# Requesting the q weights earlier and in two pieces: the order of the first loads in a fused attention and GLU kernel

## The chip, the cores and the metric

One core of a Trainium2 chip. The metric is the time of one execution on the device in microseconds (us), lower is better; medians of several runs are quoted with their range. The span in a profile is some 1.7 us shorter than the time of the same run, because it counts from the first to the last instruction. Ratios are computed as the mean time of one kernel's fast runs over the mean of the other's of the same rounds, so they are not quite the ratio of the medians quoted beside them.

## The reference, cut to what matters

A layer norm of x (2048 rows of 512, bf16), then a local dilated attention (32 heads of 16, eight keys for each position) and a gated GLU on the same normalized x, combined at the end:

```python
x = A_x
xn = _layernorm(x, axis=-1)
s = _A_ref(xn, A_wqkv, A_wo)                      # q, k, v projections, attention, wo
g = _silu(_B_ref(xn, B_w_gate, B_w_up, B_w_down)) # gelu(xn@wg) * (xn@wu) @ wd
return x + s * g
```

For this change only the beginning matters: the first 512 rows of x (tiles 0 to 3 of 128 rows) must be loaded, normalized and transposed, and the q and k weights (the first two 512-column blocks of `wqkv`, 512 KB each) must be there, before TensorE can project.

## The kernel before: the parts concerned

All loads are issued by one queue in this order (cut):

```python
    def load_w(dst, src, lo, hi):
        nc.sync.dma_start(
            out=dst[:, :, lo:hi], in_=src.rearrange("(k p) n -> p k n", p=P)[:, :, lo:hi]
        )

    for t in range(TPQ - 1):
        load_x(t)                       # x tiles 0, 1, 2: 128 KB each
    load_w(wqkv_sb, A_wqkv, 0, D)       # q weights: 512 KB
    load_x(TPQ - 1)                     # x tile 3
    for i in range(1, 3):
        load_w(wqkv_sb, A_wqkv, i * D, (i + 1) * D)   # k, v weights
    load_x(TPQ, TPQ)                    # x tiles 4 to 7
    ...                                 # GLU weights and the rest of x
```

And the beginning of the compute (cut). `project` makes the matmuls, four row blocks (`dks`) of weights for each group; `transpose` transposes a normalized tile on TensorE and copies the result out of PSUM:

```python
    first_moments(0); first_moments(1)          # one statement a line in the kernel
    first_normalize(0)
    transpose(0)
    first_normalize(1)
    warm_up(4, P)
    transpose(1, parts=2)                       # copied out by ScalarE, in two parts
    warm_up(4, P)
    first_moments(2); first_moments(3)
    first_normalize(2); first_normalize(3)
    ...
    for dks in ((0, 1), (2, 3)):                # q for tiles 0 and 1
        for fo in range(NC):
            project(qs[fo], wqkv_sb, fo * P, 0, 0, HQ, dks)
    for fo in range(NC):
        qkv(0, fo, 0, HQ, qs[fo])
    transpose(HT, copy=nc.vector.tensor_copy)   # tile 2
    for fo in range(NC, 2 * NC):                # k for tiles 0 and 1
        qkv(0, fo, 0, HQ)
        if fo == NC:
            transpose(HT + 1, copy=nc.vector.tensor_copy)   # tile 3
    ...
    for fo in range(2 * NC):                    # q and k for tiles 2 and 3
        qkv(0, fo, HQ, HQ)
```

The softmax here doesn't subtract the row's maximum and nothing guards it: scores larger than these inputs give would overflow.

Of the kernel before, what the change touches and what calls it, by code (L numbers as in the profile page):

```python
# [13 lines left out]
P = 128  # L14
# [14 lines left out]
def kernel(  # L29
# [13 lines left out]
    nc = tc.nc  # L43
    B, S, D = A_x.shape
    DF = B_w_gate.shape[1]
    NT, NC, NF, NJ = S // P, D // P, DF // P, S // TQ
    TPQ = TQ // P
# [28 lines left out]
    wqkv_sb = wts.tile([P, NC, 3 * D], BF16, name="wqkv_sb")  # L76
# [7 lines left out]
    def load_x(t, n=1):  # L84
        nc.sync.dma_start(  # L85
            out=x_sb[:, t : t + n, :],
            in_=x2d[t * P : (t + n) * P, :].rearrange("(t p) d -> p t d", p=P),
        )

    def load_w(dst, src, lo, hi):  # L90
        nc.sync.dma_start(
            out=dst[:, :, lo:hi], in_=src.rearrange("(k p) n -> p k n", p=P)[:, :, lo:hi]
        )

    for t in range(TPQ - 1):
        load_x(t)
    load_w(wqkv_sb, A_wqkv, 0, D)
    load_x(TPQ - 1)
    for i in range(1, 3):
        load_w(wqkv_sb, A_wqkv, i * D, (i + 1) * D)  # L100
    load_x(TPQ, TPQ)
    for i, (lo, hi) in enumerate(((0, DF // 2), (DF // 2, DF))):
        load_w(wg_sb, B_w_gate, lo, hi)
        load_w(wu_sb, B_w_up, lo, hi)
        load_x((2 + i) * TPQ, TPQ)

    def load_late_weights():
# [16 lines left out]
        out=vT.rearrange("(k p) n -> p k n", p=P)[:, :, 0:PAD],  # L124
        in_=zpad[:],
# [82 lines left out]
    def transpose(t, parts=1, copy=None):  # L208
        xn = xns[t]
        tr = mm.tile([P, NC * P], BF16, name="tr", tag="mm")  # L210
        for c in range(NC):
            nc.tensor.transpose(tr[:, c * P : (c + 1) * P], xn[:, c * P : (c + 1) * P], ident[:])  # L212
        j, i = divmod(t, TPQ)
        if i == 0:
            xnT[j] = xtp.tile([P, NC, TQ], BF16, name="xnT")
        dst = xnT[j][:, :, i * P : (i + 1) * P]
        src = tr[:].rearrange("p (c n) -> p c n", c=NC)
        for k in range(parts):
            c = slice(k * NC // parts, (k + 1) * NC // parts)
            if copy is None:  # L220
                nc.scalar.activation(out=dst[:, c], in_=src[:, c], func=AF.Copy)  # L221
            else:
                copy(out=dst[:, c], in_=src[:, c])

    def warm_up(n, cols):

        ps = mm.tile([P, TQ], F32, name="warm_ps", tag="mm")
        for _ in range(n):
            nc.tensor.matmul(
                ps[:, 0:cols], lhsT=nc.const_aps.tensor(1.0, [P, P], BF16),  # L230
                rhs=nc.const_aps.tensor(1.0, [P, cols], BF16), start=True, stop=True,
            )
# [24 lines left out]
    def qkv(j, fo, i0=0, n=TQ, ps=None):  # L257
        which, c = divmod(fo, NC)
        if fo == 0 and i0 == 0:
            st[j]["q"] = qp.tile([P, NC, TQ], BF16, name="q_sb")  # L260
        if ps is None:
            ps = mm.tile([P, n], F32, name="qkv_ps", tag="mm")[:]
            project(ps, wqkv_sb, fo * P, j, i0, n)
        if which == 0:
            nc.scalar.activation(out=st[j]["q"][:, c, i0 : i0 + n], in_=ps, func=AF.Copy)  # L265
        elif which == 1:
            lo = PAD + j * TQ + i0
            nc.scalar.activation(out=k_sb[:, c, lo : lo + n], in_=ps, func=AF.Copy)  # L268
        else:
            vst = sm4.tile([P, TQ], BF16, name="vst")  # L270
            nc.scalar.activation(out=vst[:], in_=ps, func=AF.Copy)  # L271
            lo = PAD + j * TQ
            nc.sync.dma_start(out=vT[c * P : (c + 1) * P, lo : lo + TQ], in_=vst[:])
# [174 lines left out]
    for i in range(TPQ):  # L448
        at(("qkv", 0, i), normalize, TPQ + i)
        at(("glu", 0, 7 + i), moments, 2 * TPQ + i)  # L450
        if i < 2:
            at(("glu", 0, i), transpose, TPQ + i)
        at(("glu", 0, 8 + i), normalize, 2 * TPQ + i)
        at(("glu", 1, 0), transpose_by_dma, 2 * TPQ + i)
        at(("glu", 1, 10 + i), moments, 3 * TPQ + i)
        at(("qkv", 2, 2 * i), normalize, 3 * TPQ + i)
        at(("glu", 2, 0), transpose_by_dma, 3 * TPQ + i)
# [31 lines left out]
    HT = TPQ // 2  # L489
# [4 lines left out]
    first_moments(1)  # L494
    first_normalize(0)
    transpose(0)
    first_normalize(1)
    warm_up(4, P)
    transpose(1, parts=2)
    warm_up(4, P)  # L500
    first_moments(2)
    first_moments(3)
# [7 lines left out]
            project(qs[fo], wqkv_sb, fo * P, 0, 0, HQ, dks)  # L510
    for fo in range(NC):
        qkv(0, fo, 0, HQ, qs[fo])
    transpose(HT, copy=nc.vector.tensor_copy)
    for fo in range(NC, 2 * NC):
        qkv(0, fo, 0, HQ)
        if fo == NC:
            transpose(HT + 1, copy=nc.vector.tensor_copy)
    for t in range(TPQ, 2 * TPQ):
        moments(t)
    sum_constants()  # L520
# [49 lines left out]
```

## Time and profile before

| | before |
|---|---|
| time, us | 230.13 (230.06 to 230.57, three runs) |
| span of the profiled run | 228.7, of a run of 230.45 |
| TensorE busy | 98% of the span |
| q weights complete | 6.95 us |
| k weights complete | 8.80 us |
| first q matmul | 7.00 us |

The profiled run is one of the slower ones of its range.

The beginning in three stretches. This is the windows view of the kernel before; the columns are the stretch, its length, then for each engine its busy time and number of instructions, the granted clock, the DMA engines' busy share and GB/s:

```profile
6.00:6.95 0.95, 0.28 (x5) 0.10 (x2) 0.38 (x2) 0.93 (x4) 0.00 (x0) 1.00 1.08 376
7.00:8.80 1.80, 1.80 (x16) 1.48 (x16) 1.37 (x5) 0.30 (x1) 0.00 (x0) 1.00 1.09 345
8.80:10.00 1.20, 1.20 (x17) 1.11 (x16) 0.93 (x4) 1.05 (x4) 0.00 (x0) 1.00 1.10 354
```

TensorE is idle for most of the stretch before 6.95, where it waits for the q weights, and not at all in the two behind it.

### The profile page before, as it was taken

The numbers are of one execution on the slowest core, as the hardware profiler recorded it, in microseconds if no ns is written. First come the engines' busy times: TensorE is split into PE (matmuls) and PEld (weight loads), VectorE is DVE, ScalarE is ACT, GpSimd is POOL, SyncE is SP. The second block draws the span as 40 slices with busy tenths as digits, with TensorE's granted clock in tenths as the row PEclk, the third lists the DMA queues.
The fourth block names the chain that finished last, engine by engine and source line by source line (L and its number), as shares of the span: only waits on it lengthen the run. The fifth ranks groups of instructions, "written<-read, shape, count | busy, mean of one in ns | idle before, by whom it ended". The sixth has DMA issues, their size and how long they took to land.

```text
span 228.7 us, 3538 instructions
## 1 busy us (share of the span) xinstructions
PE 223.6 (98%) x1324; PEld 106.3 (46%) x1324; DVE 147.6 (65%) x234; ACT 130.2 (57%) x214; POOL 23.0 (10%) x61
## 2 busy tenths in 40 slices
PE   8899999999999999999999999999999999999993
PEld 6764444444444444444444444444444444444453
DVE  4584996896995198865677169735549429945232
ACT  4679769764413866467621786747642396748211
POOL 1048973000000000110000000000000000000000
PEclk9999999999999999999999999999999999999999
DMA  6999589982378211110275711110147800000001
GB/s 163 359 373 371 140 170 199 242 204 75 109 172 197 55 24 29 26 29 0 92 175 135 170 25 28 26 34 0 45 120 165 203 26 3 0 0 4 23 23 46
DMA packets 30545, 24.46 MB, mean 107 GB/s; under 512 B 10176, under 2 KB 30528, under 8 KB 30528
## 3 DMA queue, kind: packets, MB, share of 16 engines
q1 hardware_dynamic: 30528, 24.24, 41.9%
q8 instruction: 10, 0.16, 0.3%
q14 instruction: 7, 0.06, 0.1%
HBM read 18.61 MB, written 4.31 MB: 100 GB/s over the span
## 4 chain that ended last, share of the span: by engine, by line
PE 94%; DMA 2%; ACT 1%; SPq 1%; DVE 0%; issue 0%; DVEq 0%
PE y_ps L416 21%; PE u_ps L247 21%; PE g_ps L247 21%; PE qkv_ps L247 17%; PE s_ps L426 6%; PE L_ps L304 3%; PE o_ps L375 3%; DMA wqkv_sb<-in_A_wqkv_dram 2%; PE q_ps L247 1%; ACT L400 1%; SPq L85 1%; PE den_ps L324 0%; ACT ge L400 0%; ACT vst L271 0%; PE tr L212 0%; ACT xnT L221 0%
## 5 line engine op out<-in xcount | busy, mean ns | idle before, releaser
L247 PE MATMUL g_ps<-xnT,wg_sb 128*128 128x512 bf16 x224 | 57.6, 379 | 0.0
L247 PE MATMUL u_ps<-xnT,wu_sb 128*128 128x512 bf16 x224 | 57.5, 379 | 0.0
L416 PE MATMUL y_ps<-wd_sb,h 128*128 128x512 bf16 (+1 forms) x238 | 51.2, 366 | 0.0
L404 DVE TENSOR_TENSOR h<-ge,u 128x512 bf16<-128x512 bf16 x56 | 23.8, 425 | 37.1 <-ACT u L402 36.4
L293 DVE TENSOR_TENSOR pk<-q_sb,k_sb 128x2048 bf16<-128x2048 bf16 x32 | 37.8, 1221 | 7.0 <-ACT k_sb L268 7.0
L402 ACT ACTIVATE u<-u_ps 128x512 bf16<-128x512 f32 x56 | 33.5, 599 | 14.7 <-PE u_ps L247 14.7
L400 ACT ACTIVATE ge<-g_ps 128x512 bf16<-128x512 f32 x56 | 33.5, 599 | 14.7 <-PE g_ps L247 14.4
L247 PE MATMUL qkv_ps<-xnT,wqkv_sb 128*128 128x512 bf16 (+1 forms) x208 | 40.9, 355 | 0.0
L361 DVE TENSOR_TENSOR pv<-E,v_arr 128x2048 bf16<-128x2048 bf16 x32 | 38.6, 1216 | 0.0
L416 PEld LDWEIGHTS <-h 128*128 128x128 bf16 x238 | 23.3, 98 | 25.3
L423 ACT ACTIVATE sl<-y_ps 128x512 bf16<-128x512 f32 (+1 forms) x17 | 9.7, 572 | 44.0 <-PE y_ps L416 44.0
L247 PEld LDWEIGHTS <-wu_sb 128*128 128x128 bf16 x224 | 21.9, 98 | 26.7 <-issue 0.3
L247 PEld LDWEIGHTS <-wg_sb 128*128 128x128 bf16 x224 | 21.2, 98 | 27.1 <-issue 3.0
L247 PEld LDWEIGHTS <-wqkv_sb 128*128 128x128 bf16 x224 | 21.6, 98 | 20.2 <-DMA wqkv_sb<-in_A_wqkv_dram 0.9
L434 DVE TENSOR_TENSOR m<-s_ps,sl 128x512 bf16<-128x512 f32 (+1 forms) x17 | 11.2, 658 | 24.2 <-PE s_ps L426 24.1
L426 PE MATMUL s_ps<-wo_sb,oT 128*128 128x512 bf16 (+1 forms) x68 | 16.6, 366 | 0.0
L197 POOL TENSOR_TENSOR rstd<-rstd,mhalf 128x1 f32<-128x1 f32 x12 | 7.7, 638 | 77.4 <-DVE rstd L194 75.2
L271 ACT ACTIVATE vst<-qkv_ps 128x512 bf16<-128x512 f32 x16 | 9.6, 597 | 6.4 <-PE qkv_ps L247 6.4
L268 ACT ACTIVATE k_sb<-qkv_ps 128x512 bf16<-128x512 f32 (+1 forms) x20 | 10.2, 514 | 3.5 <-PE qkv_ps L247 3.2
L265 ACT ACTIVATE q_sb<-qkv_ps 128x512 bf16<-128x512 f32 (+1 forms) x16 | 8.7, 544 | 3.6 <-PE qkv_ps L247 3.3
L426 PEld LDWEIGHTS <-oT 128*128 128x128 bf16 x68 | 6.6, 98 | 7.2
L159 POOL COPY spread<-ident 32x32 bf16<-32x32 bf16 x16 | 9.7, 646 | 0.2
(52 smaller groups left out, 115.8 us busy)
## 6 DMA issues: line engine op xcount, KB each, us to landing
v_arr<-vT SPq DMA_DIRECT2D x16, 520.0 KB, 5.1
vT<-vst SPq DMA_DIRECT2D x16, 128.0 KB, 2.1
out_dram<-o_t SPq DMA_DIRECT2D x15, 128.0 KB, 2.3
wg_sb<-in_B_w_gate_dram SPq DMA_DIRECT2D x2, 896.0 KB, 10.9
wu_sb<-in_B_w_up_dram SPq DMA_DIRECT2D x2, 896.0 KB, 12.7
wd_sb<-in_B_w_down_dram SPq DMA_DIRECT2D x1, 1792.0 KB, 13.7
wqkv_sb<-in_A_wqkv_dram SPq DMA_DIRECT2D x3, 512.0 KB, 5.6
x_sb<-in_A_x_dram SPq DMA_DIRECT2D x3, 512.0 KB, 11.4
```

The costliest lines, as they stand in the source:

```text
L159: nc.gpsimd.tensor_copy(out=spread[H * q : H * (q + 1), q, H * j : H * (j + 1)], in_=ident[H * q : H * (q + 1), H * q : H * (q + 1)],)
L247: nc.tensor.matmul(ps, lhsT=w[:, dk, lo : lo + P], rhs=xnT[j][:, dk, i0 : i0 + n], start=(dk == 0), stop=(dk == NC - 1),)
L268: nc.scalar.activation(out=k_sb[:, c, lo : lo + n], in_=ps, func=AF.Copy)
L293: nc.vector.tensor_tensor(out=pk[:], in0=st[j]["q"][:], in1=k_sb[:, :, off : off + TQ], op=ALU.mult)
L361: nc.vector.tensor_tensor(out=pv[:], in0=st[j]["E"][:, wh, :].unsqueeze(1).to_broadcast([P, 4, TQ]), in1=st[j]["va"][:, 4 * g : 4 * g + 4, ...
L400: nc.scalar.activation(out=ge[:], in_=g_ps[:], func=AF.Gelu_apprx_tanh)
L402: nc.scalar.activation(out=u[:], in_=u_ps[:], func=AF.Copy)
L404: nc.vector.tensor_tensor(out=h[:], in0=ge[:], in1=u[:], op=ALU.mult)
L416: nc.tensor.matmul(y[:], lhsT=st[j][fc][:, tt * P : (tt + 1) * P], rhs=wd_sb[:, fc, cols], start=(fc == 0), stop=(fc == NF - 1),)
L423: nc.scalar.activation(out=sl[:, cols], in_=y[:], func=AF.Silu)
L426: nc.tensor.matmul(s[:], lhsT=st[j]["oT"][:, g, tt * P : (tt + 1) * P], rhs=wo_sb[:, g, cols], start=(g == 0), stop=(g == NC - 1),)
L434: nc.vector.tensor_tensor(out=m[:], in0=s[:], in1=sl[:, cols], op=ALU.mult)
```

## The change

Its intent: let the q matmuls start earlier. The q weights move ahead of x tiles 2 and 3, in two requests (row blocks 0 and 1, then 2 and 3), so that the first half of the q matmuls needs only the first request. x tiles 2 and 3 come in one request behind them. The copy of transposed tile 1, which the q matmuls need too, is split between VectorE and ScalarE. As tile 2 now comes later, its transposes move behind the first k block.

```diff
-    def load_w(dst, src, lo, hi):
+    def load_w(dst, src, lo, hi, k0=0, k1=NC):
         nc.sync.dma_start(
-            out=dst[:, :, lo:hi], in_=src.rearrange("(k p) n -> p k n", p=P)[:, :, lo:hi]
-        )
-
-    for t in range(TPQ - 1):
-        load_x(t)
-    load_w(wqkv_sb, A_wqkv, 0, D)
-    load_x(TPQ - 1)
+            out=dst[:, k0:k1, lo:hi],
+            in_=src.rearrange("(k p) n -> p k n", p=P)[:, k0:k1, lo:hi],
+        )
+
+    load_x(0)
+    load_x(1)
+    load_w(wqkv_sb, A_wqkv, 0, D, 0, 2)
+    load_w(wqkv_sb, A_wqkv, 0, D, 2, 4)
+    load_x(2, 2)
...
-            if copy is None:
+            if copy is None or k % 2:
...
-    transpose(1, parts=2)
+    transpose(1, parts=2, copy=nc.vector.tensor_copy)
...
-    transpose(HT, copy=nc.vector.tensor_copy)
     for fo in range(NC, 2 * NC):
         qkv(0, fo, 0, HQ)
-        if fo == NC:
-            transpose(HT + 1, copy=nc.vector.tensor_copy)
+        if fo < NC + 2:
+            transpose(HT + fo - NC, copy=nc.vector.tensor_copy)
```

## The prediction

> **What bounds the kernel now.** I read, in this order: the page's busy shares, the chain that ended last in order of time, the timeline and waits of the first 12 us, and the windows view.
>
> The busy shares say TensorE:
>
> ```profile
> PE 223.6 (98%) x1324; PEld 106.3 (46%) x1324; DVE 147.6 (65%) x234; ACT 130.2 (57%) x214; POOL 23.0 (10%) x61
> ```
>
> That leaves 228.7 - 223.6 = 5.1 us of TensorE idle time in the whole span. The windows view shows where it is not:
>
> ```profile
> 24.00:200.00 176.00, 176.00 (x999) 78.36 (x998) 121.87 (x176) 103.53 (x161) 13.45 (x28) 1.00 0.41 93
> ```
>
> From 24 to 200 us TensorE has work in every moment, at clock 1.00. So a start that is earlier or later by d moves the end by d, and nothing in the middle absorbs it. The change touches only the first 12 us, so only those need to be read. The chain there:
>
> ```profile
> 0.80 0.39 SPq L85
> ...
> 1.25 0.42 SPq L85
> ...
> 1.71 0.43 SPq L85
> 2.14 0.04 issue
> 2.19 4.76 DMA wqkv_sb<-in_A_wqkv_dram
> 6.95 0.05 issue
> 7.00 1.92 PE q_ps L247 x16
> 8.91 0.31 PE tr L212 x4
> 9.22 0.44 PE qkv_ps L247 x4
> 9.66 0.22 PE tr L212 x4
> 9.88 8.27 PE qkv_ps L247 x60
> ```
>
> The first q matmul waits for the q weights (512 KB), whose request waits behind three x requests of 0.4 us each on the queue. They land at 6.95. After that the chain is TensorE alone. The timeline shows what stands close behind it:
>
> ```profile
> 6.99 1.64 PEld L247 LDWEIGHTS <-wqkv_sb 128*128 128x128 bf16 x16 [0.89 <-DMA wqkv_sb<-in_A_wqkv_dram]
> 7.00 1.92 PE L247 MATMUL q_ps<-xnT,wqkv_sb 128*128 128x256 bf16 x16 [0.72 <-DMA wqkv_sb<-in_A_wqkv_dram]
> 7.36 0.69 DVE L181 BATCH_NORM_STATS2 stats<-x_sb 128x6 f32<-128x512 bf16 x1 [0.95 <-DMA x_sb<-in_A_x_dram]
> 8.82 0.23 PEld L212 LDWEIGHTS <-xn 128*128 128x128 bf16 x4 [0.19 <-DVE xn L203]
> 9.06 0.60 PE L247 MATMUL qkv_ps<-xnT,wqkv_sb 128*128 128x256 bf16 x4
> 9.72 8.42 PE L247 MATMUL qkv_ps<-xnT,wqkv_sb 128*128 128x256 bf16 x60
> ```
>
> TensorE loses 0.72 us to the q weights. VectorE has x tile 3 only at 7.36, and tile 2's statistics (at 5.51) were finished long before. The q matmuls end as tile 2's transposes come ready: 0.19 us of waiting there. So the whole prize of an earlier q start is under one microsecond, 0.4% of the time, and other arrivals stand 0.2 us behind it.
>
> **What the Trainium skill says.** (1) "DMA: Bandwidth & Descriptors", section "Queues, rings and completion order": each DMA engine takes descriptors in ring order, and a request is complete only when all engines have counted. The trace agrees: requests land in issue order, at 2.85, 3.50 and 3.88 (x tiles 0 to 2), 6.95 (q weights), 7.34 (x tile 3), 8.80 (k weights); of the sixteen completion counts of the q weights fifteen are in by 6.32 and the last at 6.95. So order in the queue is what decides. (2) The same page, "Anatomy of one DMA", gives about 2 us fixed cost for one request (for another issuing path); here an x tile takes 2.0 to 2.2 us from issue to landing, so a second request costs nothing extra while the queue is full. (3) "VectorE: DVE Perf Modes", section "Why PSUM operands drop a tier": a PSUM operand allows at most two results a cycle. The 128x512 copies here took 424 ns, under the 533 ns that one per cycle at the page's 0.96 GHz would take: it agrees; half the columns is an estimated 424 - 133 = 290 ns. (4) "TensorE: Matmul & The Clock Gate", Part 1: the clock falls only after some 3.4 us of idleness. The granted clock is 1.00 in every window here, with the 0.72 us gap in it; the gaps expected below are shorter than 1 us, so no clock is lost.
>
> **The change part by part.**
>
> *Queue order.* Before: x0, x1, x2, q, x3, k. After: x0, x1, qA, qB, x2+x3, k; five requests ahead of k in both, so the issue time is the same. In the packet records 256 KB are done at 2.95 and 384 KB at 3.49: x2 took 0.54 us. The q weights move forward by that: complete at 6.95 - 0.54 = 6.41. Once the queue is full 128 KB takes 0.35 us, so half A (256 KB less) lands about 0.73 earlier, 5.7.
>
> *x tiles 2 and 3.* All bytes up to x3 are the same 1024 KB. x2's 128 KB now pass at the full rate (0.35 in place of 0.54), so the pair lands at 7.34 - 0.19 = 7.15 and k at 8.80 - 0.19 = 8.6. For x3 that is a gain of 0.2, but x2, which was there at 3.88, now comes at 7.15.
>
> *Copy of tile 1.* Before: ScalarE, 6.09 to 6.47 and 6.37 to 6.75. After: the first half on VectorE. Tile 1's transposes end at 6.05; tile 2's copy began 0.04 after its transposes, so 6.09 to 6.38. The built instruction order shows ScalarE's half waiting for VectorE's half: 6.40 to 6.78. It isn't shared in time; but the second half is needed only by the ninth q matmul, which comes at 6.43 + 8 x 0.109 = 7.30. q starts at 6.43 in place of 7.00: **0.57 gained**, bound by the copy now, not the weights.
>
> *What follows q.* q's 16 matmuls take 16 x 0.109 = 1.75: done at 8.18 (before 8.75). The next is now the first k block; k weights are there at 8.6, so TensorE waits 0.45, and the block runs 8.65 to 9.09. Then tile 2's transposes. They need the chain stats 2, aggregate, stats 3, aggregate, square root, reciprocal, normalize, all after 7.15. The same chain ran for tiles 0 and 1: from 2.87 to the first transposes at 5.13, 2.26 us. So 7.17 + 2.26 = 9.43: another 0.34 of waiting. Then 0.24 (transposes), 0.44 (second k block), 0.24 (tile 3's transposes, ready about 0.5 after tile 2's): the third k block starts at 9.43 + 0.92 = 10.35. Before, it started at 9.72 + 0.44 = 10.16. **Net: 0.2 later.** The gain of 0.57 is paid back as 0.45 + 0.34 of new waits, against 0.19 removed at the old transposes (rounding apart, a debt of 0.2).
>
> *ScalarE.* Its queue holds the square roots of tiles 2 and 3 ahead of the q evictions. For tiles 0 and 1 the second root ended 2.04 after the first statistics began, so now at 7.17 + 2.04 = 9.2, and the q evictions run 9.2 to 10.45 (before 8.95 to 10.16, 1.21 for four), the first k eviction to 10.85. The fourth k block waits for that PSUM buffer and wants to start at 10.79: a tie, worth up to 0.1. Thus 230.13 + 0.2 = 230.3.
>
> **The rivals.**
>
> *The gain survives.* If the queue's slow start (102 GB/s between 3.5 and 4.4, against 372 from 5 on) mostly vanishes with the new order, the pair lands at 6.8 and k at 8.3. Then q, two k blocks and both transposes run 6.43 + 1.75 (8.18), k at 8.35, transposes at 9.1, third k block at 10.0: 0.15 gained, 230.0. For it: x2's slow 0.54 is removed. Against: the slow start sits at the first packets of the q weights (400 to 870 ns each in the packet records, against 46 normally), which still come.
>
> *The pair is late.* Two completions in one: if the last DMA engine lags more, the pair lands at 7.5, the third k block starts at 10.7, and ScalarE's evictions add to it: 230.7. For it: the last count lagged by 0.63 already. Against: that lag is in x3's 7.34 already.
>
> *Hidden anyway.* If a later wait ended before the rest of the kernel followed TensorE, nothing would move: 230.1. x tiles 4 to 7 land at 11.80 and are far from TensorE's path; the wait at 21.2 is for ScalarE's table load, which itself follows TensorE. So I think the shift passes through.
>
> **Range and chances.** The three endings are 230.0, 230.3 and 230.7; runs of the kernel before spread over 230.06 to 230.57. I take 230.3, with 229.7 to 230.9 for eight in ten. Two per cent would be 4.6 us, more than all of TensorE's idle time before 24 us: faster 0.01, same 0.98, slower 0.01.
>
> **What would show it.** Right: q matmuls starting at 6.4 and waiting for VectorE's copy; a new wait of TensorE for the k weights around 8.2 to 8.6; a wait of its weight loads for xn until about 9.4; glu's first matmul later than 18.20 by 0.0 to 0.4. Wrong if q still waits for the weights after 6.6, if the pair's statistics begin outside 6.9 to 7.4, or if the rest of the kernel doesn't carry the shift of the first 11 us to its end.

## The result, and the profile after

| | before | after |
|---|---|---|
| time, us, six runs each | 230.12 (229.93 to 230.57) | 231.36 (230.62 to 231.72) |
| ratio of the fast runs | | 1.0047 (95%: 1.0026 to 1.0068) |
| span of the profiled run | 228.7 | 230.0 |
| first q matmul | 7.00 | 6.64 |
| k weights complete | 8.80 | 9.61 |
| third k block starts | 10.16 | 11.33 |

The change makes the kernel slower by 0.5%, or 1.1 to 1.2 us (by the ratio, or by the medians). Within 2% that counts as the same, as forecast, but it is outside the range forecast in us. The busy shares of the page first:

```profile
PE 222.6 (97%) x1304; PEld 106.3 (46%) x1324; DVE 147.7 (64%) x235; ACT 129.9 (57%) x213; POOL 21.7 (9%) x61
```

No engine has more work than before (1304 matmul records in place of 1324 are records missing from the trace: the weight loads are all there). The difference is waiting. The chain that ended last, of the changed kernel, in order of time (start, duration, what):

```profile
1.71 0.43 SPq L91
2.14 0.04 issue
2.19 0.47 SPq L91
2.66 0.04 issue
2.70 5.43 DMA x_sb<-in_A_x_dram
8.13 0.02 issue
8.15 0.70 DVE stats L184
...
9.94 0.42 DVE xn L206
10.37 0.05 issue
10.41 0.40 PE tr L215 x4
10.81 0.44 PE qkv_ps L250 x4
```

Before, this chain ran over the q weights and then over TensorE alone until 18.15. Now it runs over the x pair, which is complete only at 8.13, and over VectorE's work on it until 10.41. TensorE's timeline shows both waits (start, duration, line, operation, how often; in brackets the idle time before it and what ended it):

```profile
6.64 1.91 PE L250 MATMUL q_ps<-xnT,wqkv_sb 128*128 128x256 bf16 x16 [0.25 <-DVE xnT L226]
9.66 0.61 PE L250 MATMUL qkv_ps<-xnT,wqkv_sb 128*128 128x256 bf16 x4 [1.11 <-DMA wqkv_sb<-in_A_wqkv_dram]
10.41 0.40 PE L215 MATMUL tr<-ident,xn 128*128 128x128 bf16 x4
10.65 0.60 PE L250 MATMUL qkv_ps<-xnT,wqkv_sb 128*128 128x256 bf16 x4
11.08 0.39 PE L215 MATMUL tr<-ident,xn 128*128 128x128 bf16 x4
11.33 7.98 PE L250 MATMUL qkv_ps<-xnT,wqkv_sb 128*128 128x256 bf16 x55
```

q does start earlier, at 6.64, and no longer waits for weights. Then TensorE waits 1.11 us for the k weights and some 0.3 us for tile 2. The same windows as before:

```profile
6.00:6.95 0.95, 0.70 (x10) 0.53 (x8) 0.29 (x1) 0.66 (x2) 0.00 (x0) 1.00 1.00 309
7.00:8.80 1.80, 1.55 (x15) 1.14 (x12) 0.65 (x1) 0.00 (x0) 0.00 (x0) 1.00 0.98 308
8.80:10.00 1.20, 0.34 (x4) 0.31 (x4) 1.09 (x6) 0.40 (x2) 0.00 (x0) 1.00 0.98 323
```

TensorE gains 0.4 us in the first stretch and loses 1.1 in the other two. The last column is the new thing: 308 to 323 GB/s where the kernel before moved 345 to 376. The bytes and the queue are the same, but in this stretch they come more slowly. Earlier it is the other way round: the windows view gives 247 GB/s from 1.5 to 5 us, where the kernel before had 191, and over 1.5 to 7 us the two are level (253 and 257). So both kernels have a slow phase; with the change it falls later, when the x pair and k are under way.

The DMA view's issue line for the k weights (size, us from issue to landing), issued at 3.21 in both kernels, says it in one number. Before, and then after:

```profile
wqkv_sb<-in_A_wqkv_dram SPq DMA_DIRECT2D x1, 512.0 KB, 5.6
```

```profile
wqkv_sb<-in_A_wqkv_dram SPq DMA_DIRECT2D x1, 512.0 KB, 6.4
```

The trace records sixteen completion counts for each of these requests, and they show where that time lies. For the k weights of the kernel before, fifteen counts come between 7.57 and 8.18 and one at 8.80. For the changed kernel eleven come between 7.28 and 8.06, and five between 8.74 and 9.61. The x pair is the same: twelve by 6.18, the last at 8.13. The mean of k's sixteen counts has hardly moved, from 8.01 to 8.06; the last has, from 8.80 to 9.61. So most DMA engines deliver no later than before; some lag, and a request is complete with the last.

### The profile page after: what moved, and what is told of

Its sections match the earlier page's. It is cut to its first block, busy times and chain, and to the rows that moved or that the text cites. A ratio compares the mean times of both kernels' runs of the same rounds, so it can differ in the third digit from the quotient of the medians.

```text
span 230.0 us, 3519 instructions
## 1 busy us (share of the span) xinstructions
PE 222.6 (97%) x1304; PEld 106.3 (46%) x1324; DVE 147.7 (64%) x235; ACT 129.9 (57%) x213; POOL 21.7 (9%) x61
## 4 chain that ended last, share of the span: by engine, by line
PE 92%; DMA 2%; ACT 2%; DVE 1%; issue 1%; SPq 1%; ACTq 0%; DVEq 0%
PE y_ps L419 21%; PE u_ps L250 21%; PE g_ps L250 20%; PE qkv_ps L250 17%; PE s_ps L429 6%; PE L_ps L307 3%; PE o_ps L378 3%; DMA x_sb<-in_A_x_dram 2%; DVE stats L184 1%; ACT L403 1%; ACT u L405 1%; PE den_ps L327 0%; SPq L91 0%; SPq L85 0%; PE tr L215 0%
## 5 line engine op out<-in xcount | busy, mean ns | idle before, releaser
L250 PE MATMUL g_ps<-xnT,wg_sb 128*128 128x512 bf16 x213 | 56.3, 379 | 0.5 <-issue 0.2
L390 DVE TENSOR_TENSOR oT<-o_ps,rbd 128x1024 bf16<-128x1024 f32 x6 | 7.1, 1218 | 2.9 <-DMA rbd<-rs_d 2.9
```

Source lines behind the costliest of these rows:

```text
L250: nc.tensor.matmul(ps, lhsT=w[:, dk, lo : lo + P], rhs=xnT[j][:, dk, i0 : i0 + n], start=(dk == 0), stop=(dk == NC - 1),)
```

## The experiments

I had one reading for everything behind 12 us, and it is checked first, because it turns each trace into a time: the time of the profiled run minus the start of the third k block is 220.26 to 220.41 us in all twenty traces. Whatever happens in the first 11 us passes to the end one for one. (The third k block is the first matmul that has both q, two k blocks and both of the late tiles' transposes behind it.)

The traces hold the DMA packets, and I use one more number from them: how many 1 KB packets that started between 5 and 7 us took over 120 ns; 46 ns is usual. It is 0 in the kernel before and 21 in the changed one. It says when, not how many in all: from 1.5 to 5 us the kernel before has 35 such packets and the changed one 29. All runs together, in the order of the text:

| run | q weights | time, median (range) | ratio to before (95%) | k complete | slow packets, 5 to 7 us | third k block |
|---|---|---|---|---|---|---|
| before | whole | 230.12 (229.93 to 230.57) | 1 | 8.80 | 0 | 10.16 |
| changed | split | 231.36 (230.62 to 231.72) | 1.0047 (1.0026 to 1.0068) | 9.61 | 21 | 11.33 |
| e1 | split | 231.24 (230.62 to 231.62) | 1.0044 (1.0031 to 1.0056) | 8.89 | 17 | 10.29 |
| e2 | split | 231.49 (230.29 to 232.06) | 1.0057 (1.0032 to 1.0082) | 9.01 | 21 | 10.40 |
| e3 | split | 231.24 (231.18 to 232.10) | 1.0058 (1.0043 to 1.0073) | 9.47 | 10 | 10.87 |
| e4 | whole | 230.33 (230.25 to 230.77) | 1.0010 (0.9998 to 1.0022) | 8.42 | 2 | 9.96 |
| f1 | whole | 230.27 (230.05 to 230.76) | 1.0007 (0.9995 to 1.0019) | 8.19 | 2 | 9.77 |
| f2 | whole | 230.41 (230.26 to 231.33) | 1.0018 (1.0004 to 1.0031) | 8.16 | 4 | 9.85 |
| f3 | split | 231.44 (230.67 to 231.89) | 1.0048 (1.0035 to 1.0061) | 9.67 | 16 | 11.53 |
| f4 | split | 231.09 (230.54 to 231.74) | 1.0041 (1.0028 to 1.0055) | 9.71 | 22 | 10.86 |
| g1 | split | 231.11 (230.92 to 231.37) | 1.0040 (1.0028 to 1.0053) | 9.63 | 14 | 11.02 |
| g2 | whole | 230.34 (230.31 to 230.93) | 1.0007 (0.9993 to 1.0021) | 8.91 | 1 | 10.60 |
| g3 | split | 230.73 (230.43 to 230.98) | 1.0022 (1.0010 to 1.0035) | 8.86 | 15 | 10.17 |
| h1 | whole | 230.71 (one run) | | 9.08 | 2 | 10.41 |
| r1 | whole | 230.70 (230.30 to 231.76) | 1.0029 (1.0012 to 1.0045) | 8.76 | 7 | 10.15 |
| r2 | whole | 231.45 (231.23 to 232.30) | 1.0063 (1.0049 to 1.0077) | 9.84 | 2 | 11.52 |
| r3 | split | 230.90 (230.74 to 231.09) | 1.0032 (1.0020 to 1.0044) | 7.66 | 13 | 10.51 |
| r4 | whole | 233.65 (233.53 to 235.05) | 1.0153 (1.0140 to 1.0166) | 8.48 | 0 | 14.64 |
| s1 | whole | 230.15 (229.95 to 231.20) | 1.0002 (0.9985 to 1.0019) | 8.90 | 2 | 10.29 |
| s2 | whole | 230.51 (230.21 to 231.01) | 1.0009 (0.9995 to 1.0023) | 8.78 | 0 | 10.46 |

The last three columns are of the one profiled run of each, so they carry the chance of that run; the times are of five or six runs.

**First group: again, and one part changed.** My theory after the result was that the new queue order lets some DMA engines lag (A). The rivals: the lag is chance and the new order merely lost the slack that hid it (B); the cost lies in the chain of VectorE behind the joined request for x tiles 2 and 3; or in the shared copy.

*e1*, the changed kernel again without an edit:

> The changed kernel again, unaltered, for a second trace. In its first trace the x pair landed at 8.13 and the k weights at 9.61, a microsecond later than forecast, with four of the sixteen completion counts lagging. Theory A (the order of the queue makes those engines lag): pair again at 7.8 to 8.4, k at 9.3 to 9.8, time 231.0 to 231.7. Theory B (the lag is chance, the new order only removed the slack that hid it): pair and k land anywhere between 7.1 and 8.4 and 8.6 and 9.8, and the start of the third k block moves with them one for one.

The second trace fell on the fastest run of the set, 230.62, and shows what the prediction had worked out:

```profile
6.96 1.91 PE L250 MATMUL q_ps<-xnT,wqkv_sb 128*128 128x256 bf16 x16 [0.25 <-DVE xnT L226]
8.94 0.61 PE L250 MATMUL qkv_ps<-xnT,wqkv_sb 128*128 128x256 bf16 x4
9.39 0.39 PE L215 MATMUL tr<-ident,xn 128*128 128x128 bf16 x4
9.61 0.60 PE L250 MATMUL qkv_ps<-xnT,wqkv_sb 128*128 128x256 bf16 x4
10.05 0.39 PE L215 MATMUL tr<-ident,xn 128*128 128x128 bf16 x4
10.29 1.91 PE L250 MATMUL qkv_ps<-xnT,wqkv_sb 128*128 128x256 bf16 x16
```

Here the pair was complete at 7.06 and k at 8.89, and the third k block starts at 10.29, against 7.15, 8.6 and 10.35 forecast. So how far the engines lag varies from run to run, as B says, but the changed kernel's usual run (231.2 to 231.4) has more of it than this one, and its fastest is slower than the slowest of six of the kernel before. Both theories have a part.

*e2*, x tiles 2 and 3 in two requests, and *e3*, tile 2 normalized before tile 3's statistics:

```diff
-    load_x(2, 2)
+    load_x(2)
+    load_x(3)
```

> The changed kernel with x tiles 2 and 3 in two requests again, at the same place in the queue. If the joined request costs by making tile 2's statistics wait for tile 3 (a serial chain of 2.3 us after the landing instead of 1.5), the first transposes of the second half come 0.7 to 0.8 after nearer to x tile 3's landing, and the time falls by 0.3 (where k's landing then holds TensorE) to 0.8 us. If the joined request doesn't matter: no change, within 0.2 us.

```diff
     first_moments(2)
-    first_moments(3)
     first_normalize(2)
+    first_moments(3)
     first_normalize(3)
```

> The changed kernel, but tile 2 is normalized before tile 3's statistics are taken. If the chain on VectorE is what delays TensorE, tile 2's transposes start 1.5 after the pair's landing instead of 2.3; tile 3's come at 2.9 to 3.0 after it instead of 2.75. The third k block waits for both, so the time should stay within 0.2 us: a gain of 0.5 or more would say that only the first transposes matter.

Neither helps: 231.49 and 231.24. For e2 that is the "no change" branch; in e3 it is as expected. In e3's trace the k weights end at 9.47, TensorE waits for them until 9.52, and tile 2's transposes follow at 9.96 with no wait of their own. VectorE's chain is the last wait in some runs and the k weights in others; shortening only one of them leaves the other.

*e4*, the kernel before with the shared copy alone:

```diff
-            if copy is None:
+            if copy is None or k % 2:
...
-    transpose(1, parts=2)
+    transpose(1, parts=2, copy=nc.vector.tensor_copy)
```

> The kernel before with the shared copy of tile 1 alone. q then still waits for its weights at 6.95, so the time should be that of before within 0.15 us, and the first q matmul at 7.0. If the copy itself cost something, q would start later than 7.0 by the difference.

230.33, a ratio of 1.0010 whose interval includes 1: the copy is not the loss. The trace brought something else. With the queue order of before, q's weights landed at 6.28 here, all sixteen counts within 0.7 us, and q started at 6.61, not at the 7.0 expected. The wait until 6.95, on which the prediction (and the change's intent) rested, came from one late count in one trace.

**Second group: the parts of the queue order.**

*f1*, the changed kernel with the queue order of before:

```diff
     load_x(0)
     load_x(1)
-    load_w(wqkv_sb, A_wqkv, 0, D, 0, 2)
-    load_w(wqkv_sb, A_wqkv, 0, D, 2, 4)
-    load_x(2, 2)
+    load_x(2)
+    load_w(wqkv_sb, A_wqkv, 0, D)
+    load_x(3)
```

> The changed kernel with the queue order of before (x0, x1, x2, q in one request, x3, k), the shared copy and the first k block ahead of tile 2's transposes kept. Theory A (the new queue order costs, by late and unevenly landing x pair and k weights): k lands at 8.4 to 8.8 again, the third k block starts at 10.0 to 10.2, and the time is that of before within 0.2 us, 229.9 to 230.3. Rival (the moved transposes or the copy cost): the time stays at 231.0 or more.

230.27: the loss is gone, and the copy and the moved transposes are still in. The loss is in the queue. *f2* takes back only the split:

```diff
-    load_w(wqkv_sb, A_wqkv, 0, D, 0, 2)
-    load_w(wqkv_sb, A_wqkv, 0, D, 2, 4)
+    load_w(wqkv_sb, A_wqkv, 0, D)
     load_x(2, 2)
```

> The changed kernel with the q weights in one request at their new place. If the extra request (the split) is what spreads the completion counts, k lands at 8.6 to 8.9 with at most one late count and the time falls to 230.3 to 230.6. If it is the place in the queue, ahead of x tile 2: late counts again (k at 8.9 to 9.6) and 231.0 to 231.5.

230.41, with k complete at 8.16, earlier than either branch had it, and its counts within 0.6 us. TensorE's timeline of f2:

```profile
6.66 1.91 PE L249 MATMUL q_ps<-xnT,wqkv_sb 128*128 128x256 bf16 x16 [0.24 <-DVE xnT L225]
8.40 0.60 PE L249 MATMUL qkv_ps<-xnT,wqkv_sb 128*128 128x256 bf16 x4
8.93 0.40 PE L214 MATMUL tr<-ident,xn 128*128 128x128 bf16 x4
9.17 0.60 PE L249 MATMUL qkv_ps<-xnT,wqkv_sb 128*128 128x256 bf16 x4
9.60 0.39 PE L214 MATMUL tr<-ident,xn 128*128 128x128 bf16 x4
9.85 2.34 PE L249 MATMUL qkv_ps<-xnT,wqkv_sb 128*128 128x256 bf16 x20
```

With q whole the k weights are there when q is done, at 8.40, where the changed kernel waits until 9.66. *f4* makes the same test from the other side: the old order and the shared copy (e4), with q split at its old place.

```diff
     load_x(2)
-    load_w(wqkv_sb, A_wqkv, 0, D)
+    load_w(wqkv_sb, A_wqkv, 0, D, 0, 2)
+    load_w(wqkv_sb, A_wqkv, 0, D, 2, 4)
     load_x(3)
```

> The kernel before with the shared copy and the q weights in two requests, at their old place behind x tile 2. One request more stands ahead of x3 and k (some 0.45 us of issue), but the queue is full by then, so if requests cost only issue time nothing moves: q at 6.6 to 7.0, k at 8.4 to 8.9, 230.0 to 230.4. If a second request for the same weights spreads the completion counts, k lands after 9.0 and the time is over 230.7.

231.09, k at 9.71, and the wait is back:

```profile
9.75 0.61 PE L249 MATMUL qkv_ps<-xnT,wqkv_sb 128*128 128x256 bf16 x4 [0.27 <-DMA wqkv_sb<-in_A_wqkv_dram]
```

So the split costs, at the new place as at the old: the ratios differ by 1.0047 - 1.0018 = 0.0029 (changed and f2) and by 1.0041 - 1.0010 = 0.0031 (f4 and e4), 0.7 us in both. Taken together, the quoted intervals leave some 0.6 us of doubt on the first and 0.4 on the second. A third pair, e2 and r1 below, which again differ in the split alone, gives 1.0057 - 1.0029 = 0.0028, but with 0.7 us of doubt.

The slow packets separate the traces without overlap: 10 to 22 in the nine with q split, 0 to 7 in the eleven with q whole. They do not rank the times: g3 has 15 and takes 230.73, r2 has 2 and takes 231.45.

*f3* puts tile 2's transposes back ahead of the first k block:

> The changed kernel with tile 2's transposes ahead of the first k block again. Where the k weights land before the transposes come ready (pair + 2.3 us), the move had filled that wait with a k block: without it the third k block should start 0.2 to 0.45 us later, time up by that, 231.4 to 231.8. Where the k weights are the last to land, the order costs nothing and the time stays at 231.2.

231.44 against 231.24 to 231.36: no difference that these runs could show. In its trace TensorE waits 1.68 us for tile 2 in one piece, in place of two shorter waits.

**Third group: why the split spreads the counts.**

*g1*, q in two requests of 64 partitions, all four row blocks in each:

```diff
-    load_w(wqkv_sb, A_wqkv, 0, D)          # as in f2
+    for p0 in (0, P // 2):
+        nc.sync.dma_start(
+            out=wqkv_sb[p0 : p0 + P // 2, :, 0:D],
+            in_=A_wqkv.rearrange("(k p) n -> p k n", p=P)[p0 : p0 + P // 2, :, 0:D],
+        )
```

> The changed kernel with the q weights in two requests of 64 partitions each (all four row blocks in each) in place of two requests of 128 partitions and two row blocks. If it is two smaller requests as such that spread the later completion counts: k at 8.9 to 9.7, 230.9 to 231.5. If it is the two row blocks for each partition: k at 8.1 to 8.4 as with one request, 230.2 to 230.5.

231.11, k at 9.63: the time is that of a split along row blocks, but the trace is not. One count of k is late here, and the other fifteen lie together, 8.54 to 8.96, all later than in f2 (7.63 to 8.16). The queue took 0.78 and 0.65 us over the two requests of 64 partitions, against 0.48 and 0.51 in the changed kernel, so k was requested at 3.79 only (f2: 2.73, changed: 3.21). How much of g1's loss is this later request is not separated, so g1 doesn't show that the dimension is of no matter.

*g2*, q whole and the k weights in two requests, and *g3*, the changed kernel with k in two requests as well:

```diff
-    for i in range(1, 3):
-        load_w(wqkv_sb, A_wqkv, i * D, (i + 1) * D)
+    load_w(wqkv_sb, A_wqkv, D, 2 * D, 0, 2)
+    load_w(wqkv_sb, A_wqkv, D, 2 * D, 2, 4)
+    load_w(wqkv_sb, A_wqkv, 2 * D, 3 * D)
```

> The changed kernel with q in one request and the k weights in two (row blocks 0 and 1, then 2 and 3). If any weights request of two row blocks upsets what follows: k or v late by 0.5 or more, 230.7 or more. If only the first large request meets the slow first packets (q's here) and all behind it run at full rate: k at 8.1 to 8.4, v at 9.6, 230.2 to 230.5.

> The changed kernel with the k weights in two requests as well. If the slow packets come with the first request of four row blocks, which is k's in the changed kernel, then they move on to v, which nobody waits for before 14 us: k at 8.1 to 8.5, time 230.2 to 230.6. If the split of q by itself slows what follows, k stays late, 8.9 to 9.7, and 231.0 to 231.5.

g2 takes 230.34 and has one slow packet: splitting the later request costs nothing that these runs could show (its profiled run, 230.93, is the slowest of its five, with k at 8.91 by one late count). g3 takes 230.73, between the two branches, and its slow packets stay where they were (15 from 5 to 7 us), which speaks against the idea that they come with the first large request. That idea is not confirmed; g3 is inconclusive.

*h1*, the kernel before again:

> The kernel before, unaltered, for a second trace. Its first trace is of a run of 230.45, near the top of its range (229.93 to 230.57), with one late count: q at 6.95 where fifteen counts were in by 6.32. If that late count is chance, q lands at 6.2 to 6.4 here, q's matmuls start at 6.5 to 6.8 already and the run takes 229.9 to 230.2. If it belongs to the kernel: 6.9 and 7.0 again.

The chance branch did not come out: q at 7.22 with one late count (fifteen by 6.28), in a run of 230.71, just over the range of the nine runs beside it (229.98 to 230.59). Of the five traces with the old order and q whole (before, h1, e4, f1, s1) three have q's last count at 6.95 to 7.22 and two at 6.28 and 6.33. The late count comes and goes with the run, in the same kernel or in one whose queue is the same.

**Fourth group: number of requests, and when they are issued.**

*r1*, q whole, x tiles 2 and 3 apart (as many requests as the changed kernel), and *r2*, q whole and x tile 0 split:

> The changed kernel with q in one request and x tiles 2 and 3 in two: six requests up to and with k's, as in the changed kernel. If the number of requests ahead of k spreads the counts: k at 8.9 to 9.7, 230.9 or more. If the split of q does: k at 8.1 to 8.9 with at most one late count, and, as tile 2's statistics no longer wait for tile 3, 229.9 to 230.4.

```diff
-    load_x(0)
+    for p0 in (0, P // 2):
+        nc.sync.dma_start(out=x_sb[p0 : p0 + P // 2, 0, :], in_=x2d[p0 : p0 + P // 2, :])
     load_x(1)
```

> q in one request at its new place, x tile 0 in two requests of 64 partitions. Everything behind is issued 0.45 us later, and tile 0 is complete 0.3 to 0.5 later, so q starts at 7.0 to 7.2 and the time is 230.6 to 230.9 if nothing else happens and the counts of k stay together (at most one late). If any extra early request spreads the counts: k at 9.2 to 9.9 with several late, 231.2 or more.

r1 lands between its branches: 230.70, k at 8.76, its counts evenly spread over 1.0 us, seven slow packets. Whether one more request ahead of k has an effect by itself is not shown: the intervals of r1 and f2 overlap. The number of requests alone can't be the cause, as the kernel before, e4 and f1 also have five ahead of k, as the changed kernel has, with k requested at the same 3.21. r2 is slow, 231.45, for another reason: the two half requests took the queue 0.63 us each, so q was requested at 2.69 in place of 1.71 (0.45 had been reckoned), its weights come at 7.58 and q starts only at 7.62. k's last count, 9.84, is 0.5 behind the next, with two slow packets. It tells little of the split.

*r3* and *r4*, x tiles 0 and 1 issued from ScalarE's queue, so that the weights are requested 0.9 us earlier; q split in r3 and whole in r4:

```diff
-    load_x(0)
-    load_x(1)
+    load_x(0, queue=nc.scalar)
+    load_x(1, queue=nc.scalar)
```

> The changed kernel, x tiles 0 and 1 issued by ScalarE's queue, so that q's two requests, the pair and k are issued 0.9 us earlier. If the engines' late counts are waits for descriptors issued too late: counts stay together, k at 7.8 to 8.4, and the time is 229.8 to 230.5. If not: several late counts of k again (8.6 to 9.5), 230.6 to 231.3.

> As the run before, with q in one request. x tiles 0 and 1 share the engines with q now and may land 0.2 to 0.6 later, which delays the first q matmul by as much; k at 7.7 to 8.3. If the x tiles' delay is small, this beats the kernel before: 229.6 to 230.0; if it is 0.5, 230.2 to 230.5.

In r3 the counts stay together: k from 7.18 to 7.66, the earliest of all kernels, although q is split. That is what a lag caused by requests issued too late would do. But x tiles 0 and 1 are late, q starts at 7.42 and the time forecast was missed (230.90). r4 went wrong in an unforeseen way: tile 1 was complete at 6.23 only, behind the q weights (5.84), and TensorE idled until 7.71. Its timeline:

```profile
7.71 0.61 PE L214 MATMUL tr<-ident,xn 128*128 128x128 bf16 x4 [2.45 <-DVE xn L205]
9.65 3.57 PE L249 MATMUL q_ps<-xnT,wqkv_sb 128*128 128x256 bf16 x16
13.74 0.39 PE L214 MATMUL tr<-ident,xn 128*128 128x128 bf16 x4
```

q's sixteen matmuls take 3.57 us, and 1.91 or 1.92 in every other kernel; four transposes take 0.61 and, from 13.74 on, 0.39 again. In the trace the warm-up matmuls (256 columns) start 213 ns apart until 4.6 us and 107 ns apart for the last four; after the 2.45 us of idleness those of q start 213 ns apart again, and from 13.6 us on the spacing is 109. So TensorE ran at half speed from 7.71 to about 13.5 us. The windows view gives the granted clock as 1.00 from 4 to 16 us, but that is no measurement: this run's clock record begins at 13.59, and the view counts time without a record as full speed. From the first transposes to the third k block r4 takes 14.64 - 7.71 = 6.93 us, f2 9.85 - 5.26 = 4.59: 2.3 us of its delay fall in this slow stretch, and 2.45 are the late tiles. (The profiled run, 235.05, is the slowest of r4's six; the others took 233.53 to 233.73.)

**Fifth group: is there anything to keep?** *s1* is the kernel before with only the first k block ahead of tile 2's transposes (f1 without the shared copy); *s2* is f2 without the shared copy.

> The kernel before with the first k block ahead of tile 2's transposes, and nothing else of the change. Its twin with the shared copy took 230.27. If the shared copy delays q's start (6.6 to 6.7 there, while ScalarE's first half ends at 6.47 in the kernel before), this starts q at 6.5 to 6.6 unless a late count holds it, and takes 229.9 to 230.1. If the copy costs nothing: 230.2 to 230.3.

> The changed kernel with q in one request and tile 1's copy on ScalarE alone. Its twin with the shared copy took 230.41. If the shared copy costs 0.1 to 0.2: 230.2 to 230.3; if nothing: 230.4. If q's weights at their new place are worth something against the kernel before: under 230.0.

s1 takes 230.15 and s2 230.51, with ratios whose intervals include 1. s2 starts q at 6.67 with the copy on ScalarE, f2 at 6.66 with the shared one: the shared copy gains nothing and costs nothing. No version here beats the kernel before by more than the noise.

**What is settled and what is not.** Shown: the loss is in the queue, and about 0.7 us of it come with the split of the q weights. What the traces show beside it are slow packets after 5 us and some counts of the x pair and k that come late; that the slow packets make the counts late is not shown by an experiment. What is left of the loss, the 1.0018 of f2, is not settled: s2 and g2, which have the q weights whole at the same place, have 1.0009 and 1.0007, with intervals that include 1. Not shown: why the split does this. That descriptors come too late for requests that the engines reach too early would fit r3, and r1 in part, but g3 and the slow packets that r3 still has (13) don't speak for it, and r3 also delayed the x tiles. It stays open.

## Why the prediction was wrong

*The bound and the passing on of a shift.* Right: 220.26 to 220.41 us from the third k block to the end in every trace, whatever happened before.

*Copy of tile 1.* Right in kind and duration: VectorE's half took 293 ns (6.20 to 6.49; 290 estimated), ScalarE's half waited for it (6.52 to 6.91). q started at 6.64 and not at 6.43, because x tile 0 came 0.1 later in that run and TensorE's first weight load started 0.12 after the copy's end.

*The q weights.* Both halves came far earlier than forecast, at 4.49 and 5.20 in place of 5.7 and 6.4. The prediction expected the slow first packets to stay in front of q. They did not: they appeared later, between 5 and 7 us, on the requests behind. The rival "the gain survives" had named this slow start but not that it could move.

*The chain behind the pair.* Right: 10.41 - 8.15 = 2.26 us from the first statistics to the first transposes, as forecast.

*The step that failed* is the sentence that "a second request costs nothing extra while the queue is full", and with it the landings "at 7.34 - 0.19 = 7.15" and "8.80 - 0.19 = 8.6". The second request for q was reckoned at nothing, and measured at about 0.7 us. The landings were 8.13 and 9.61 in the first trace and 7.06 and 8.89 in the second; with q in one request (f2) they were 6.65 and 8.16, so without the split the forecast would have been on the late side. That the old lag was "in x3's 7.34 already" was the reason given against the rival of a late pair; with the split there is more of it. The rival was the right one, and even its 230.7 was too low.

*A second, smaller error is in the base.* The prediction worked the third k block out as 10.35, and 10.35 + 220.33 = 230.7. It wrote 230.3, because it took the difference to the 10.16 of the trace (a run of 230.45) and added that to the median of all runs (230.13). Those belong to different runs: the median run of the kernel before has its third k block at about 230.12 - 220.33 = 9.8. Of the 231.36 - 230.3 = 1.1 us missed, 0.35 are this, and the rest, 0.7, is about the size measured for the split. That this closes so well is partly luck: 9.8 is inferred and not seen in a trace of a median run, and f2, without the split, took 230.41 and not the 230.7 of the corrected sum.

*A slip in the cross-check.* The bracket after "Net: 0.2 later" doesn't add up: 0.57 - 0.45 - 0.34 + 0.19 leaves a debt of 0.03. The 0.19 is the idle time of the weight loads; the matmuls had waited only 8.82 - 8.75 = 0.07. The sum over the blocks, 10.35 against 10.16, is right.

*ScalarE's tie* was not seen: no wait for a PSUM buffer ended any idle time of TensorE there.

## What to carry to other kernels

Splitting an early transfer so that its first half can be used sooner can delay the transfers behind it; look at all sixteen completion counts of the next requests, not only at the one that was moved up. Before acting on a wait in one trace, compare that run's time with the median and look at a second trace: here the wait of 0.72 us was a late count that two of five traces of that queue order did not have. And take a difference only between numbers of the same run.

## What the Trainium skill lacked or had wrong

- "DMA: Bandwidth & Descriptors" doesn't say that dividing one request in two can slow the requests behind it. Here 512 KB of q weights in two requests cost about 0.7 us (f2 against the changed kernel, e4 against f4), with 10 to 22 packets over 120 ns between 5 and 7 us against 0 to 7.
- The same page says that the completion semaphore counts up to sixteen engines, but gives no size for their spread. In the kernel before, the last count of the q weights came 0.63 us after the fifteenth in one trace and 0.94 in another (6.28, then 7.22); in the changed kernel five of sixteen counts of k were 0.7 to 1.6 us behind the eleventh.
- "TensorE: Matmul & The Clock Gate" has the clock fall after a window of about 3.4 us of idleness. In r4 a gap of 2.45 us was enough (the fast spacing had begun only 0.6 us before it): sixteen matmuls took 3.57 us in place of 1.91, and the slow stretch lasted nearly 6 us. Gaps of 0.72 to 1.68 us in the other runs did nothing of the kind.
